# A decayed linear attention with an MLP behind it: batch 0's diagonal sums as products on TensorE, its decay tables by doubling, a tiled U^T x, and a planner that starts each engine at its own time

## The chip, the cores and the metric

The kernel runs on one core of a Trainium2 chip. The metric is the device time of one execution in microseconds (us); the median of three runs of the kernel before is 419.65 us (419.59 to 420.86). One execution was also taken by the hardware profiler, and all rows of the profile come from that one.

TensorE is called PE below, VectorE DVE, ScalarE ACT, GpSimd POOL and SyncE SP, as in the profile. SP and ACT issue the DMAs.

## The reference

Two stages follow each other. The first is a linear attention with a decaying state, for 4 batches, 8 heads, 768 time steps and a head size of 48:

```python
for t in range(S):
    kt, vt, rt = (k[:, :, t], v[:, :, t], r[:, :, t])
    cur = np.einsum('bhd,bhe->bhde', u[None] * kt, vt)
    y[:, :, t] = np.einsum('bhd,bhde->bhe', rt, state + cur)
    state = w[None, :, :, None] * state + np.einsum('bhd,bhe->bhde', kt, vt)
```

The term with `u` is the diagonal: the row t of y gets v_t times the number sum_d r_t[d] u[d] k_t[d], one such number for each head and step.

The second stage takes x, the attention's result with the heads side by side (768 rows of 384 per batch), adds a mixing over time of rank 32, and an MLP of width 1536:

```python
xt = x.transpose(0, 2, 1)
h = xt @ U @ V
u = x + h.transpose(0, 2, 1)
ch = np.maximum(u @ w_ch1, 0.0) @ w_ch2
return (u + ch).astype(np.float32)
```

All arithmetic is float32. The four arrays of the second stage arrive as 64-bit floats, seen by the kernel as pairs of 32-bit words.

## The kernel before, in words

**Attention.** The 768 steps of a batch are cut in 6 chunks of 128 rows, a chunk in two halves of 64. Heads go in pairs: a pair's 2 x 48 channels lie on partitions 0 to 47 and 64 to 111 (PD = 112 rows). For a chunk n, r and k are loaded row by row (`a_load`), turned by PE (`a_tr`, 128x128 transposes into a PSUM bank, tiles `ptr` and `ptk`) and scaled by tables of powers of w as they are copied out (rT on DVE, kT on DVE or ACT). `ks` is k times another table, `tab` (`a_ks`). A chunk is computed in two parts (`a_part`): each has 64x64-tiled matmuls of the chunk n itself (`pav`: masked scores `am` times v, and rT times the state S) interleaved with those of the chunk n + 1 (`pab`: scores, and the state's increment). Part 1 may start when ACT or DVE has read one element of part 0's bank (`seen`). Between parts DVE masks the scores (`am`, L967), adds the increments into the state (`S`, L995), and somebody multiplies the state by the decay (`SW`, L1004 or L1008). So chunk n + 1 cannot start its part 0 before part 1 of chunk n, its `am` and its `S`, and before rT and kT of chunk n + 2 are there. The very first matmuls (`a_first`) are the scores and increments of chunk 0 alone.

The diagonal is computed beside it: r times k, times `ub` (u on all partitions), each a 128x384 product (`a_dv`, L713 and L715, on POOL for batch 0), a sum over the 48 channels on DVE (`a_dg`, L721), and v times that sum with 8 small ACT instructions a chunk (L725). `a_x` (L974) adds it to the bank of `pav` and gives x.

**Tables.** w is loaded transposed, 4 bytes at a time (`load_w`, L415 and L417), clipped, and powers of it and of its reciprocal are built on DVE (`tables`, L437 to L460). One of them, `tw`, is turned by PE (L465) and becomes `tab` (L467).

**From x to the MLP.** For batch 0, `c_gx` adds each chunk's U^T x to columns 128 to 511 of the PSUM bank `wake`, with three full 128x128 matmuls a chunk that use three copies of U side by side; `c_g0` splits the sum into high and low parts (`Gs`). For the other batches `c_g` does the whole sum in one go, with 24 matmuls on four 32-column tiles (`pG`, L1040; a float32 product leaves two rows in the trace, so 48), and gathers the four blocks by four small copies first. `c_x` turns x into the banks `pu`, `c_xu` adds V^T Gs there, and ACT and DVE split the result into `uTh` and `uTl`.

**MLP.** For a block of 384 rows and a slice f of 128 hidden channels, `m_1` has 9 matmuls of 384 columns (three split products by three 128-row pieces), ACT takes relu into `hh` (L1162), DVE the rest into `hl` (L1163), and `m_2` has 9 more. Batch 0's slices go in the order t0 f0-3, t1 f0-7, t0 f4-11, t1 f8-11, since the weights come in meanwhile. Each weight slice, 64-bit, has to be converted: 8 bits of exponent by DVE (L540) or ACT (L544), the rest scaled by ACT (L566), sign and join on DVE (L547, L550), a high part by ACT (L584), a low part by DVE or POOL (L585). The last stores of `out` are issued by `m_2` (L1207).

**The order of the work.** Nothing is left to a compiler: each step is an `op` with an engine (or several to choose from, `one_of` and `on_either`), a cost in ns, what it reads and writes, and a key. The key is a due time in us that the code at the end of `rwkv_moe` gives (`T0` and `PER` for the MLP, `FRONT` and `EACH` for batch 0's chunks). `Plan.schedule` simulates the engines with these costs, picks among what is ready the smallest key, and so fixes the order of every engine's queue; at run time each engine works through its queue in order and waits on semaphores. Where PE would be idle, the plan fills in matmuls of an identity (`wake`), so that PE's clock stays up; they sit in the queue too, ahead of what follows.

While batch b is in its MLP, the attention of batch b + 1 is woven between its matmuls. Only batch 0's attention has nothing to be woven into.

Of the kernel before, what the change touches and what calls it, by code (L numbers as in the profile page):

```python
# [20 lines left out]
W_LO = 0.7  # L21
# [26 lines left out]
class Plan:  # L48
# [7 lines left out]
    LANDS = 1650  # L56

    CROWD, CROWDED = 1.29, 32000
# [20 lines left out]
    def op(self, eng, ns, fn, w=(), r=(), alt=(), lock=False, dma=0.0, rows=0, late=0.0, tiled=False, dk=0.0):  # L79
# [11 lines left out]
        for acc, write in [(a, False) for a in r] + [(a, True) for a in w]:  # L91
            b, sub = acc if isinstance(acc, tuple) else (acc, None)
            if not b.uses and b.tag:
                o.allocs.append(b)
                ring = self.rings.setdefault(b.tag, {"order": [], "next": 0, "free": [(0.0, "")] * b.bufs, "last": None})
# [53 lines left out]
    def schedule(self):  # L149
        free = dict.fromkeys(self.AFTER, 0.0)  # L150
# [49 lines left out]
        while left:  # L200
            best = None
            for e, cs in cands.items():
# [9 lines left out]
                for t, o, i in sorted((a for a in at if a[0] <= now + 1), key=lambda a: a[1].key):  # L212
# [13 lines left out]
            if e == "PE":  # L226
                for begin, end, filler in self.wakes:
# [4 lines left out]
                    while self.pe_end(x, begin.ways[0][1], 0, False) < t - 150:  # L232
# [46 lines left out]
def dve(n):  # L279
    return 130 + 1.09 * n  # L280
# [11 lines left out]
def rwkv_moe(ctx: ExitStack, tc: tile.TileContext, r, k, v, w, u, U, V, w1, w2, out):  # L292
# [20 lines left out]
    NR = 2  # L313
    NK = 2
# [75 lines left out]
    wT = cbuf([PD, NP, 1], F32, "wT")  # L390
# [3 lines left out]
    tabT = cbuf([PD, 2, NP, C2 + 2], F32, "tabT")  # L394
    wi = cbuf([PD, NP, 1], F32, "wi")
    wm = cbuf([PD, NP, 1], F32, "wm")
    tab = cbuf([128, DM], F32, "tab")

    Uf = cbuf([128, NCH, 3, R], F32, "Uf")
# [14 lines left out]
    def load_w():  # L414
        dma(lambda q: q.dma_start(wT.t[:HP, :, 0], bass.AP(tensor=w.tensor, offset=w.offset, ap=[[1, HP], [2 * D, NP]])),  # L415
            [(wT, 0)], [], HP * NP, 4, ns=730)
        dma(lambda q: q.dma_start(wT.t[HP:, :, 0], bass.AP(tensor=w.tensor, offset=w.offset + D, ap=[[1, D], [2 * D, NP]])),  # L417
            [(wT, 1)], [], D * NP, 4, ns=580)
# [4 lines left out]
    def table(i):  # L423

        return tabT.t[:, i, :, i:i + C2].unsqueeze(2).broadcast_to([PD, NP, 2, C2])
# [4 lines left out]
    def tables():  # L430

        HC = C2 // 2
        NS = HC.bit_length()
        sq = cbuf([PD, 2, NP, NS], F32, "sq")
        tt = tabT.t
        pw = tt[:, :, :, HC:C2]
        on_dve(4, lambda e: e.tensor_scalar(wT.t, wT.t, W_LO, W_HI, ALU.max, ALU.min), [wT], [])  # L437
        op("POOL", 500, lambda: nc.gpsimd.memset(pw[:, :, :, 0:1], 1.0), [tabT], [])
        on_dve(4, lambda e: e.tensor_copy(sq.t[:, 0, :, 0:1], wT.t), [sq], [wT])
        for i in range(1, NS):  # L440
# [1010 lines left out]
```

## Time and profile before

| | us |
|---|---|
| median of three runs | 419.65 |
| the profiled execution's own time | 420.94 |
| span of its trace, first to last instruction | 419.1 |
| first matmul of attention (`a_first`) | 12.07 |
| part 0 of the last chunk of batch 0 | 42.78 |
| first matmul of the MLP | 52.39 |
| last matmul of the MLP ends about | 413.2 |
| PE busy, of the span | 408.1 (97%) |
| DVE busy | 263.9 (63%) |
| ACT busy | 134.8 (32%) |
| POOL busy | 74.6 (18%) |

How to read it: the two times of the second and third row are of one execution, and 1.84 us lie around the span. Busy time of PE counts the `wake` matmuls, which compute nothing. The time marks in the middle are starts of instructions in the chain of work that ended last. A row of the view by windows gives a stretch, its length, then the busy time and the number of instructions of PE, PE's weight loads, DVE, ACT and POOL, the granted clock of PE (1.00 is full), a share of DMA time, and GB/s. A row of a timeline or of the chain gives start, length, engine, line and tile.

### The profile page before, as it was taken

To read this page: it belongs to the slowest core of one execution; us is meant where nothing else is said; L and a number is where in the kernel's file an instruction comes from. 1 tells how busy PE (TensorE), PEld (TensorE's weight loads), DVE (VectorE), ACT (ScalarE), POOL (GpSimd) and SP (SyncE) were. 2 spreads that over 40 slices of the span, in tenths; PEclk is the share of its full clock that TensorE was granted. 3 is DMA by queue.
4 is the path that set the end of the run, shared out by engine and by line. 5 is a ranking of instruction groups with operands and counts; after the bars stand their busy time and mean duration, and the time that the engine had idled before them with its cause. 6 is when DMAs were issued, how large, how long until landed. Compare 5 with 4: busy or idle time off the path is not lost.

```text
span 419.1 us, 12257 instructions
## 1 busy us (share of the span) xinstructions
PE 408.1 (97%) x5164; PEld 393.3 (94%) x5164; DVE 263.9 (63%) x594; ACT 134.8 (32%) x358; POOL 74.6 (18%) x114
## 2 busy tenths in 40 slices
PE   8998999999999999999999999999999999999994
PEld 8887999999999898999999999999999999999993
DVE  6878998889898559877784358866523361122122
ACT  2467967547641415212113130112113121111110
POOL 2642150145621103321000003321000000000000
PEclk9999999999999999999999999999999999999998
DMA  9978969899557677755677814520100510001001
GB/s 145 149 160 256 201 163 242 125 224 234 94 85 154 142 144 132 149 103 87 137 140 107 152 68 64 101 39 2 59 2 0 114 57 2 0 2 58 2 0 61
DMA packets 181951, 43.53 MB, mean 104 GB/s; under 512 B 168961, under 2 KB 180354, under 8 KB 181890
## 3 DMA queue, kind: packets, MB, share of 16 engines
q1 hardware_dynamic: 176706, 41.21, 49.1%
q10 hardware_dynamic: 5184, 1.48, 2.0%
q8 instruction: 42, 0.69, 0.7%
q14 instruction: 19, 0.16, 0.1%
HBM read 36.18 MB, written 6.49 MB: 102 GB/s over the span
## 4 chain that ended last, share of the span: by engine, by line
PE 91%; DVE 4%; ACT 2%; issue 1%; POOL 0%; DVEq 0%; ACTq 0%; POOLq 0%
PE p L347 72%; PE wake L347 3%; PE pav L836 3%; PE pav L842 3%; PE pab L795 3%; PE pab L810 2%; PE pu L347 2%; PE ptk L756 1%; PE pG L1040 1%; PE pav L821 1%; DVE am L967 1%; PE ptr L756 1%; ACT dv L725 1%; DVE SW L1004 1%; DVE ut L1136 1%
## 5 line engine op out<-in xcount | busy, mean ns | idle before, releaser
L347 PE MATMUL p<-uTh,w1s 128*128 128x384 f32 x576 | 147.5, 336 | 0.0
L1163 DVE SCALAR_TENSOR_TENSOR hl<-p,hh 128x384 fp32r<-128x384 f32 x96 | 53.2, 555 | 114.9 <-ACT hh L1162 114.5
L347 PE MATMUL p<-w2s,hh 128*128 128x384 f32 x576 | 119.9, 340 | 0.5 <-ACT hh L1162 0.4
L1162 ACT ACTIVATE hh<-p 128x384 fp32r<-128x384 f32 x96 | 47.2, 491 | 222.8 <-PE p L347 220.2
L347 PEld LDWEIGHTS p<-uTh,w1s 128*128 128x128 f32 x576 | 103.2, 188 | 0.5
L347 PEld LDWEIGHTS p<-w2s,hh 128*128 128x128 f32 x576 | 100.0, 188 | 2.4 <-ACT hh L1162 1.1
L347 PE MATMUL p<-uTl,w1s 128*128 128x384 f32 x288 | 96.5, 335 | 0.0
L347 PE MATMUL p<-w2s,hl 128*128 128x384 f32 x288 | 66.1, 335 | 0.0
L347 PEld LDWEIGHTS p<-uTl,w1s 128*128 128x128 f32 x288 | 54.0, 188 | 0.3 <-DVE uTl L1095 0.3
L347 PEld LDWEIGHTS p<-w2s,hl 128*128 128x128 f32 x288 | 51.4, 188 | 0.1
L795 PE MATMUL pab<-rT,kT 48*64 48x64 f32 x768 | 30.6, 223 | 1.8 <-issue 1.0
L836 PE MATMUL pav<-vsw,am 64*64 64x48 f32 x384 | 30.4, 222 | 0.1
L842 PE MATMUL pav<-S,rT 48*64 48x48 f32 x704 | 29.5, 218 | 0.0
L836 PEld LDWEIGHTS pav<-vsw,am 64*64 64x64 f32 x384 | 25.2, 134 | 1.9 <-issue 1.0
L795 PEld LDWEIGHTS pab<-rT,kT 48*64 48x64 f32 x768 | 24.9, 134 | 2.1 <-ACT dv L725 0.8
L842 PEld LDWEIGHTS pav<-S,rT 48*64 48x64 f32 x704 | 25.8, 135 | 0.0
L836 PE MATMUL pav<-ldv,am 64*64 64x48 f32 x320 | 24.2, 221 | 0.0
L705 POOL MEMSET ks<- 128x128 f32 x24 | 4.9, 204 | 101.9 <-PE pav L842 57.0
L967 DVE TENSOR_TENSOR am<-pab,mask 128x256 f32<-128x256 f32 x48 | 19.4, 417 | 5.4 <-PE pab L810 3.9
L836 PEld LDWEIGHTS pav<-ldv,am 64*64 64x64 f32 x320 | 20.2, 134 | 2.5 <-issue 2.1
L810 PE MATMUL pab<-ldv,ks 64*48 64x48 f32 (+1 forms) x576 | 21.1, 212 | 0.0
L995 DVE TENSOR_TENSOR S<-pab,SW 112x192 f32<-112x192 f32 x40 | 14.0, 351 | 8.2 <-PE pab L810 5.5
(136 smaller groups left out, 520.2 us busy)
## 6 DMA issues: line engine op xcount, KB each, us to landing
raw_w<-in_moe_w_ch_dram SPq DMA_DIRECT2D x24, 384.0 KB, 4.7
out_dram<-x SPq DMA_DIRECT2D x21, 192.0 KB, 2.4
ldr<-in_r_dram SPq DMA_DIRECT2D x20, 192.0 KB, 3.1
ldk<-in_k_dram SPq DMA_DIRECT2D x20, 192.0 KB, 3.5
ldv<-in_v_dram SPq DMA_DIRECT2D x20, 192.0 KB, 3.9
bl<-in_r_dram SPq DMA_DIRECT2D x79, 48.0 KB, 2.6
bl<-in_k_dram SPq DMA_DIRECT2D x79, 48.0 KB, 2.4
vsw<-in_v_dram SPq DMA_DIRECT2D x42, 48.0 KB, 2.7
```

Of the source, the lines that this page charges most:

```text
L347: return nc.tensor.matmul(*args, **kw)
L705: op("POOL", 250, lambda: nc.gpsimd.memset(ks.t[:, :, D:], 0.0), [(ks, "pad")], [])
L725: nc.scalar.activation(dv.t[:, h], vt()[:, h], AF.Copy, scale=dg.t[:, h:h + 1])
L756: nc.tensor.transpose(pt.t[:, q * C:(q + 1) * C], src().rearrange("p h d -> p (h d)")[:, q * PE_:(q + 1) * PE_], ident_)
L795: return [lambda q=q, i=i: nc.tensor.matmul(pt.t[(i ^ j) * C2:(i ^ j) * C2 + C2, q * C2:(q + 1) * C2], lhsT=kT.t[rows, q, i * C2:(i + 1) * ...
L810: return nc.tensor.matmul(pt.t[j * HP:j * HP + m, SU + q * D:SU + (q + 1) * D], lhsT=ks.t[half, 2 * q + j, :m], rhs=vt()[half, 2 * q + j, ...
L836: return nc.tensor.matmul(to(q, j, i), lhsT=am[j].t[half, q, :], rhs=vsw[n].t[half, q, :] if j else vt()[half, 2 * q, :], start=((i == 1 i ...
L842: return nc.tensor.matmul(to(q, row, i), lhsT=rT.t[rows, q, i * C2:(i + 1) * C2], rhs=St[n, i].t[rows, q, :], start=False, stop=((alone or ...
L967: on_dve(256, lambda e: e.tensor_tensor(am.t, abs_[n][j].t[:, :SU].rearrange("p (h t) -> p h t", h=NP), mask_.unsqueeze(1).broadcast_to([1 ...
L995: on_dve(192, lambda e, new=new, ptv=ptv, dec=decayed[n, j]: e.tensor_tensor(new.t, ptv(), dec.t, ALU.add), [new], [pt, decayed[n, j]])
L1162: on_act(384, lambda: nc.scalar.activation(hh.t, pt.t[:, :TB], AF.Relu), [hh], [pt])
L1163: on_dve(384, lambda e: e.scalar_tensor_tensor(hl.t, pt.t[:, :TB], 0.0, f32(hh.t), ALU.max, ALU.subtract), [hl], [pt, hh])
```

## The change

1. **Diagonal sums (batch 0).** `a_rk` multiplies rT by kT (both already turned and scaled, so that the scales cancel up to one power of w) on DVE, and four PE matmuls with 2 columns each sum it over the channels against `u2`, which holds u times w. The sums land in free columns of the `wake` bank. `a_diag` copies them out and scales v by them, on ACT or on DVE. r times k, times ub, and DVE's sum fall away for batch 0; `ub` is loaded later.
2. **Tables.** w and u come in as four rows each and are turned by PE. The powers 1 to 64 are built by doubling in six products; `tw` is read from the same powers backwards. kT of chunk 0 now comes from `ks`, like that of the others.
3. **Engines.** `ks` of chunks 2 to 5 goes to POOL, that of chunks 0 and 1 stays on DVE. The decay `SW` of batch 0 may go to POOL or ACT, no longer to DVE.
4. **U^T x.** Batch 0's is done like the others', on four 32-column tiles: chunks 0 to 3 at once, then 4 and 5; `c_g0` is gone. U is kept once, not three times.
5. **Plan.** Each engine begins at a time of its own; a held instruction may be preferred to a later one if the engine would wait little; there are somewhat fewer `wake` matmuls; the costs of DVE, of transposes in `c_turn` and of a last part are others; PER is 1.85 for 1.95; batch 0's preparation is due 3 us earlier; U and V are converted at 32 and 38 instead of both at 32; a weight's conversion is due 2 us ahead of its use instead of 6; k is loaded ahead of r and v; the flag's load waits for the last weight.
6. **End.** The middle one of the three last stores is issued by SP instead of ACT.

The diff, cut to its core:

```diff
+    BEGINS = {"DVE": 900, "ACT": 800, "PE": 1650, "POOL": 1000, "SP": 800}
+    SPARE = 0.15
-    CROWD, CROWDED = 1.29, 32000
+    CROWD, CROWDED = 1.2, 32000
+    HOLD, HELD = 3, 50000
...
-        free = dict.fromkeys(self.AFTER, 0.0)
+        free = dict(self.BEGINS)
...
+                    while e != "SP" and t < self.HELD:
+                        held = [(u, p, k) for u, p, k in at if p.key[0] < o.key[0] - self.HOLD and len(p.ways) == 1 and u > t + 1
+                                and 2 * (u - t) < o.ways[i][1] - self.OVERLAP[e] - 60]
+                        if not held:
+                            break
+                        t, o, i = min(held, key=lambda a: a[0])
...
-                    while self.pe_end(x, begin.ways[0][1], 0, False) < t - 150:
+                    until = t - 150 - (min(self.SPARE * (t - x), 600) if self.clock(x) == 1 else 0)
+                    while self.pe_end(x, begin.ways[0][1], 0, False) < until:
...
 def dve(n):
-    return 130 + 1.09 * n
+    return 163 + 1.02 * n
...
+    def load_pairs(a, t):
+        for i, (c0, c1) in enumerate(((0, HP), (HP, PD))):
+            dma(lambda q, i=i, c0=c0, c1=c1: q.dma_start(t.t[:, c0:c1], bass.AP(tensor=a.tensor, offset=a.offset + i * D,
+                                                                              ap=[[2 * D, NP], [1, c1 - c0]])),
+                [(t, i)], [], NP, 256, ns=500)
...
+        while m < C2:
+            on_dve(4 * m, lambda e, m=m: e.tensor_mul(p[:, :, m + 1:2 * m + 1], p[:, :, 1:m + 1],
+                                                      p[:, :, m:m + 1].broadcast_to([PD, NP, m])), [(pw, 1)], [])
+            m *= 2
...
-                  only="DVE" if front(n) else None)
+                  only="DVE" if n < KS else "POOL" if front(n) else None)
+
+    def a_rk(n):
+
+        rT, kT = trs[n]
+        rk = xbuf([PD, NP, C], F32, "hh", NH, f"rk_{n}")
+        on_either(512, lambda e: e.tensor_mul(rk.t, rT.t[:PD], kT.t[:PD]), [rk], [rT, kT], only="DVE" if n < RK else "POOL")
+        at_ = RKCOL + 2 * NP * n
+
+        def sums():
+            for q in range(NP):
+                whole(wk.t[:, at_ + 2 * q:at_ + 2 * q + 2], lhsT=rk.t[:, q, :], rhs=u2.t[:, q, :], start=False, stop=True,
+                      skip_group_check=True)
+        pe(480, sums, [(wk, f"d{n}")], [rk, u2])
+
+    RKCOL, RK, DIAG = 256, 6, 6
+
+    def a_diag(n):
+        vt, vb = vs[n]
+        dv = dvs[n] = xbuf([128, H, D], F32, "hh", NH, f"dv_{n}")
...
+        if n < DIAG:
+            one_of([("ACT", 1900, small, False),
+                    ("DVE", dve(384), lambda: nc.vector.tensor_mul(dv.t, vt(), dg.t.unsqueeze(2).broadcast_to([128, H, D])), True)],
+                   [dv], vb + [dg])
+            return
...
-               alt=[("DVE", dve(192), lambda one=one: one(nc.vector), True), ("ACT", NP * (act(D) - 94) + 94, four, False)])
+               alt=([] if front(n) else [("DVE", dve(192), lambda one=one: one(nc.vector), True)]) +
+               [("ACT", NP * (act(D) - 94) + 94, four, False)])
...
+    def g_sum(pt, c0, ns):
+
+        w4 = DM // 4
+        for n in ns:
+            for g in range(4):
+                nc.tensor.matmul(pt.t[g * R:(g + 1) * R, c0:c0 + w4], lhsT=Uf.t[:, n % NCH, 0],
+                                 rhs=xs[n].t[:, g * w4:(g + 1) * w4],
+                                 start=(c0 == 0 and n % NCH == 0), stop=(n % NCH == NCH - 1), skip_group_check=True)
+
+    def c_gx(*ns):
+
+        return pe(170 * len(ns), lambda: g_sum(wk, 128, ns), [(wk, "g")], [Uf] + [xs[n] for n in ns], tiled=True)
...
-                        128, 1536, ns=375, eng="ACT" if b == B - 1 and t == NTB - 1 else "SP")
+                        128, 1536, ns=375, eng="ACT" if b == B - 1 and t == NTB - 1 and i != 1 else "SP")
...
-    T0, PER = 46.0, 1.95
+    T0, PER = 46.0, 1.85
+    UV, GX, UVC = -84.9, (3, 38.6), (32.0, 38.0)
...
-        at((T0 + use[i] * PER - 6 if i > 1 else -14 + T0) + 0.01 * i, convert)
+        at((T0 + use[i] * PER - 2 if i > 1 else UVC[i]) + 0.01 * i, convert)
...
-    end = attention(0, FRONT, EACH, 1.0, 0)
+    end = attention(0, FRONT, EACH, 4.0, 0)
```

More of the change, by code (lines that the diff above doesn't have):

```diff
@@ L423, in table @@
     def table(i):
-        return tabT.t[:, i, :, i:i + C2].unsqueeze(2).broadcast_to([PD, NP, 2, C2])
+        return (tabT.t[:, :, ::-1] if i else tabT.t).unsqueeze(2).broadcast_to([PD, NP, 2, C2])
     def subs(ap):
@@ L432, in tables @@
         HC = C2 // 2
[L433 to L440, printed above, removed]
-            on_dve(4, lambda e, i=i: e.tensor_mul(sq.t[:, 0, :, i:i + 1], sq.t[:, 0, :, i - 1:i], sq.t[:, 0, :, i - 1:i]),
-                   [sq], [])
@@ new lines, in rwkv_moe, with small @@
+    RKCOL, RK, DIAG = 256, 6, 6
+    def a_diag(n):
+        vt, vb = vs[n]
+        dv = dvs[n] = xbuf([128, H, D], F32, "hh", NH, f"dv_{n}")
+        at_ = RKCOL + 2 * NP * n
+        dg = dgs[n] = wbuf([128, H], F32, "dg", 2, f"dg_{n}")
+        one_of([("ACT", 160, lambda: nc.scalar.copy(dg.t, wk.t[:, at_:at_ + H]), False),
+                ("DVE", 167, lambda: nc.vector.tensor_copy(dg.t, wk.t[:, at_:at_ + H]), False)], [dg], [(wk, f"d{n}")])
+        def small(h0=0, h1=H):
+            for h in range(h0, h1):
+                nc.scalar.activation(dv.t[:, h], vt()[:, h], AF.Copy, scale=dg.t[:, h:h + 1])
+        if n < DIAG:
[3 more added lines that the diff above has]
+            return
+        for h in range(0, H, 2):
+            op("ACT", 560, lambda h=h: small(h, h + 2), [(dv, h)], vb + [dg])
@@ L709, in a_dv @@
     def a_dv(n):
+        if front(n):
+            a_rk(n)
+            return
         (rt, rb), (kt, kb) = rs[n], ks_[n]
-        dv = dvs[n] = (xbuf([128, H, D], F32, "hh", NH, f"dv_{n}") if front(n) else
-                       wbuf([128, H, D], F32, "dv", 2, f"dv_{n}"))
-        on_either(384, lambda e: e.tensor_mul(dv.t, rt()[:, :, :D], kt()[:, :, :D]), [dv], rb + kb,
-                  only="POOL" if front(n) and n else None)
-        on_either(384, lambda e: e.tensor_mul(dv.t, dv.t, ub.t), [dv], [ub], only="POOL" if front(n) and n else None)
+        dv = dvs[n] = wbuf([128, H, D], F32, "dv", 2, f"dv_{n}")
@@ L725, in small @@
                 nc.scalar.activation(dv.t[:, h], vt()[:, h], AF.Copy, scale=dg.t[:, h:h + 1])
-        if front(n):
-            for h in range(0, H, 2):
-                op("ACT", 560, lambda h=h: small(h, h + 2), [(dv, h)], vb + [dg])
-            return
         one_of([("ACT", 1900, small, False),
@@ L747, in a_tr @@
         src, sb = (ks_ if i else rs)[n]
-        if i and n:
+        if i:
             ks = kss[n]
@@ L910, in a_part @@
         if part == 0:
-            pe(600 if last else 1000, first, wr, rd, tiled=True)
+            pe(950 if last else 1000, first, wr, rd, tiled=True)
             t = wbuf([128, 1], F32, "seen", 2, f"seen_{n}")
@@ L921, in a_part @@
         else:
-            pe(600 if last else 1000, second, wr, rd + [seens[n]], tiled=True)
+            pe(950 if last else 1000, second, wr, rd + [seens[n]], tiled=True)
         if nxt:
@@ L1389, in rwkv_moe @@
             end = attention(b, t0, per, 5.0, 0)
-        at(end, lambda b=b: c_g(b) if b else c_g0())
+        at(end, lambda b=b: c_g(b))
         if b == 0:
```

132 lines of the change are left out of this document (68 added, 64 removed).

## The prediction

> **What bounds the kernel now.** I began with the page (PE busy 97%, DVE 63%), which says little, since part of PE's work in the front is `wake`, which computes nothing. So I cut the span at the marks that the chain of waits gives, and asked the view by windows (columns: stretch, its length, then busy time and count of PE, PE's weight loads, DVE, ACT, POOL; granted clock; a DMA share; GB/s).
>
> ```profile
> 12.07:42.78 30.71, 27.97 (x779) 24.81 (x779) 24.12 (x59) 21.60 (x83) 14.10 (x24) 1.00 0.88 192
> 42.78:52.39 9.61, 9.61 (x121) 9.02 (x122) 9.00 (x19) 8.86 (x22) 1.77 (x2) 1.00 0.91 193
> 52.39:80.00 27.61, 27.61 (x163) 27.17 (x163) 26.36 (x55) 18.76 (x46) 8.17 (x10) 1.00 0.89 183
> 52.39:413.30 360.91, 360.12 (x4192) 349.21 (x4191) 221.70 (x482) 101.96 (x253) 56.17 (x76) 1.00 0.46 92
> 413.30:419.10 5.80, 0.00 (x0) 0.00 (x0) 0.43 (x1) 0.00 (x0) 0.00 (x0) 0.68 0.31 107
> ```
>
> From 52.39 on PE is idle for 0.8 us in 361, and the change takes no matmul out of that stretch. It can only be moved as a whole. So the question is how much earlier the MLP's first matmul starts, plus what the last 5.8 us give. The 52.39 us ahead of it are batch 0's attention. The chain of waits shows its last part, and PE's timeline where the chunks' parts begin:
>
> ```profile
> 12.07 0.62 PE pab L795 x32
> ...
> 41.71 0.36 DVE V L605
> ...
> 42.30 0.44 DVE am L967
> ...
> 42.78 0.67 PE pav L836 x16
> ...
> 43.91 1.92 PE wake L347 x16
> 45.83 0.60 PE pav L836 x16
> ...
> 48.70 0.90 PE wake L347 x7
> ...
> 50.82 1.10 PE pu L347 x6
> ...
> 52.39 7.77 PE p L347 x43
> ```
>
> ```profile
> 15.22 0.31 PE L836 MATMUL pav<-vsw,am 64*64 64x48 f32 x2
> ...
> 31.39 0.31 PE L836 MATMUL pav<-vsw,am 64*64 64x48 f32 x2
> ...
> 33.25 0.25 PE L836 MATMUL pav<-ld,am 64*64 64x48 f32 x1
> ...
> 36.03 0.31 PE L836 MATMUL pav<-vsw,am 64*64 64x48 f32 x2
> ...
> 39.02 1.51 PE L347 MATMUL pv<-raw_v,sel 128*96 128x192 f32 x8
> ```
>
> Part 0 of the first chunk starts at 15.22 and that of the sixth at 42.78: 27.56 us for five chunks, 5.5 each; from the fourth (31.39) to the fifth (36.03) it is 4.64, from there to the sixth 6.75. In that last one PE spreads V for 1.51 us ahead of a part, and `am` comes at 42.30 behind V's split on DVE. In the front no engine is full: DVE 79% and ACT 70% of 30.71. From 42.78 to 52.39 both are (94% and 92%), with the conversion of the weights.
>
> **The change, part by part.** *The start.* DVE's, ACT's and POOL's timelines (POOL's row is for the rule below):
>
> ```profile
> 4.57 0.17 DVE L437 TENSOR_SCALAR wT<-wT 112x4 f32<-112x4 f32 x1 [1.95 <-DMA wT<-in_w_dram]
> ...
> 4.98 0.97 DVE L441 TENSOR_TENSOR sq<-sq 112x4 f32<-112x4 f32 x5
> ...
> 8.06 0.69 DVE L457 TENSOR_TENSOR tw<-tabT,wm 112x512 f32<-112x512 f32 x1
> ...
> 15.72 1.32 DVE L1004 TENSOR_TENSOR SW<-S,wm 112x192 f32<-112x192 f32 x1
> ...
> 23.91 0.35 DVE L1004 TENSOR_TENSOR SW<-S,wm 112x192 f32<-112x192 f32 x1
> ...
> 30.83 0.69 DVE L765 TENSOR_TENSOR rT<-ptr,tabT 112x512 f32<-112x512 f32 x1 [0.30 <-PE ptr L756]
> ...
> 34.81 0.35 DVE L995 TENSOR_TENSOR S<-pab,SW 112x192 f32<-112x192 f32 x1
> ...
> 46.94 0.56 DVE L974 TENSOR_TENSOR x<-pav,dv 128x384 f32<-128x384 f32 x1 [0.47 <-PE pav L842]
> ```
>
> ```profile
> 10.08 0.48 ACT L467 COPY tab<-pt_tab 128x384 f32<-128x384 f32 x1 [6.15 <-PE pt_tab L465]
> ```
>
> ```profile
> 15.81 1.00 POOL L713 TENSOR_TENSOR dv<-ld 128x384 f32<-128x384 f32 x1
> ```
>
> w lands for DVE at 4.57 and `tw` is done at 8.75: 4.2 us. After: a clip and six products, five like the 0.194 us ones of L441 and two of up to 128 elements (0.3), then `tw` at 0.69: about 2.25 us, so 1.9 less. The load of w has 16 short rows (8 of w, 8 of u) for 448 pieces of 4 bytes, and DVE waited 1.95 us for it; but the loaded rows now go through PE first, and the one such step in these rows, from `tw` (8.75) to `tab` (10.08), took 1.33. I set the two as equal. From `tab` (10.56) to `a_first` (12.07) is 1.5 us now; kT of chunk 0 is now behind `ks` (0.55), four transposes (0.6) and a copy (0.68 on DVE): 2.0 with the hops, 0.3 to 0.5 more. Sum: **-1.5 us**; bounds +0.5 (nothing gained up to `tab`, and the longer way behind it) and -2.5 (the load gains 1). From there to the first part 0 (15.22) I leave the 3.15 us as they are.
>
> *Chunk to chunk.* What a chunk cannot go below is in the rows: part 0 to part 1 is 1.86 (31.39 to 33.25), part 1 to its last `S` another 1.9 (33.25 to 35.16), so 3.8. What it takes above that, 0.9 to 1.7, is mostly rT: at 30.83 it starts only behind its transposes, which PE did after the part; due 3 us earlier, they can go between the parts. The groups of the stretch 12.07 to 52.39 tell what each engine has to carry (busy, mean ns of one):
>
> ```profile
> L765 DVE TENSOR_TENSOR rT<-ptr,tabT 112x512 f32<-112x512 f32 x5 | 3.4, 682 | 0.3 <-PE ptr L756 0.3
> L721 DVE TENSOR_REDUCE dg<-dv 128x8 f32<-128x384 f32 x6 | 3.2, 541 | 0.0
> L1004 DVE TENSOR_TENSOR SW<-S,wm 112x192 f32<-112x192 f32 x5 | 3.5, 704 | 0.0
> L725 ACT ACTIVATE dv<-ld,dg 128x48 f32<-128x48 f32 x32 | 8.1, 326 | 3.6 <-DVE dg L721 3.5
> L715 POOL TENSOR_TENSOR dv<-dv,ub 128x384 f32<-128x384 f32 x5 | 5.5, 1094 | 0.2
> L706 DVE TENSOR_TENSOR ks<-ldk,tab 128x384 f32<-128x384 f32 x2 | 1.3, 645 | 0.0
> L771 ACT ACTIVATE kT<-ptk,wi 112x128 f32<-112x128 f32 x16 | 4.6, 367 | 1.5 <-PE ptk L756 1.5
> ```
>
> DVE loses six sums (3.2), four `ks` (4 x 0.6 = 2.4) and five `SW` (3.5), and gains six `rk` of rT's size (6 x 0.68 = 4.1): -5.0 us. ACT gains six copies of the sums (at most 0.33 each, like its other small ones) and perhaps two of the `SW` (four such each): +2 to +5. POOL loses ten products of 1.0 to 1.1 and gains four `ks` and `SW`: it is not the bound. So the diagonal is no longer work for POOL, and its sum no longer DVE's; the saving on DVE and ACT together is only 0 to 3 us, of which I take 2. The larger effect is that `seen` and rT wait less, and that V's spread (1.51) and split no longer lie ahead of parts. `rk`'s sums are 8 more rows on PE a chunk; between the tiled rows of `pG` (0.024 each, below) and the `wake` rows (0.12) that is 0.2 to 1.0 us, where PE runs `wake` matmuls now. If that cover is gone it costs up to 6 us, and it stands in the range.
>
> I take 4.8 us a chunk, nearest to the 4.64 of the undisturbed fourth, because ACT (dv 2.0, kT 1.1, `seen`, copies, `SW`) gets near 4.4. 5 x 4.8 = 24.0 for 27.56: **-3.6 us**; bounds -6.5 (4.2 a chunk) and +1 (5.7).
>
> A rule to weigh: at 15.72 one `SW` on DVE took 1.32 us while POOL ran a product (15.81), at 23.91 the same took 0.35, where POOL's timeline has no row. `rk` is a product of two SBUF tiles too, and POOL's `ks` runs beside it. If one in two collides at the 0.97 us seen here, that is 3 x 0.97 = 2.9 us on DVE, against 1.75 us of collisions that go with the `SW` (3.5 less five of 0.35); the 1.2 between them is inside what I leave open on DVE, and half a term of the range. The Trainium skill, "GPSIMD Engine Reference", section "8. Key points", says that GpSimd shares its SBUF interfaces with VectorE and contends with DVE instructions that have two SBUF inputs; the trace agrees with these two rows.
>
> *Last chunk to the MLP.* Between part 0 (42.78) and part 1 (45.83) of the last chunk are 3.05 us, of which 1.92 are U^T x; undisturbed it was 1.86. **-1.2.** At the end, Gs:
>
> ```profile
> 142.17 1.17 PE pG L1040 x48
> ...
> 145.68 0.76 PE pu L347 x3
> ```
>
> In batch 1 the tiled sum of six chunks takes 1.17 us, and from its end (143.34) to the next step (145.68) go 2.34 with the four copies. For chunk 5 alone: 0.2 + 2.34 = 2.5. Now the same is 0.90 of PE from 48.70 and 1.22 to 50.82, 2.1, but that started 1.2 after x was ready (DVE's x ends about 47.5). 50.82 - 47.5 = 3.3 against 2.5 and a hop: **-0.4**, with -1.0 and +0.5 as bounds.
>
> *The weights.* They are what comes late next. DVE and ACT carried 33.1 + 30.5 = 63.6 us in the 40.3 us from 12.07 to 52.39 (79%); with 2 less it is 61.6. With the three terms above the MLP would start at 45.7, from a start at 10.6: 35.1 us, 88%. That is tighter, but the stretch 42.78 to 52.39 ran at 93%, and a part of the conversion can go into 52.39 to 80.00, where ACT has 8.9 us and POOL 19 us idle though DVE has 1.3. I charge **+1.2**, bounds 0 and +4.
>
> *The tail.*
>
> ```profile
> L1207 ACTq DMA_DIRECT2D out_dram<-x x3: 372/389/1210, 412.7 to 414.5; - x3
> ...
> 412.13 1.60 DVE L1202 TENSOR_TENSOR x<-p,x 128x384 f32<-128x384 f32 x3 [1.00 <-PE p L347]
> ```
>
> The last store is issued at 414.5, though its x is done at 413.73, behind the second's issue of 1.21. On another queue it can go at once: 0.8 less, but the second itself then ends near 414.4 as before: **-0.6**, bounds 0 and -0.8.
>
> Sum: -1.5 - 3.6 - 1.2 - 0.4 + 1.2 - 0.6 = -6.1 us. The profiled execution took 420.94 (span 419.1 and 1.84 around it), so 414.8 for it; it lies 1.3 above the median of the runs, and on the median 419.65 the sum gives 413.5. What a measurement of this kernel can tell from no change is about 0.3%, 1.3 us.
>
> **The rivals.** *The conversion holds it.* DVE and ACT may be no better packed than now. 61.6 us at 79% of two engines are 39.0 us; from 10.6 the MLP starts at 49.6, 2.8 earlier; with the tail 3.4 gained: 416.2. For it: 94% and 92% ahead of 52.39, and conversions due 4 us later than before. Against it: the first stretch is not full, and its gaps are waits that the change addresses. Chance 0.22.
>
> *The chunks run at their floor.* 4.0 a chunk (-7.6) and no charge for weights: -11.3, 408.4. For it: the fillers and rT that go away; against: ACT near 4.4 a chunk. Chance 0.08.
>
> *PE's clock falls (slower).* The change thins the `wake` matmuls and replaces 36 full-array U^T x rows of 0.12 by short ones. The last row of the windows shows the granted clock at 0.68 once PE stands idle; everywhere else it is 1.00, as PE is kept busy. At half clock the two parts of a chunk (1.1 to 1.4 each by the rows at 31.39 and 33.25) take 2.5 us longer; from the third cold chunk on that eats the 6.1 us, and with four it is +3.9: 423.6. For it: less filling; against: the plan's own model counts PE's work per stretch, and thins only where the clock is up. Chance 0.05. The Trainium skill, "TensorE: Matmul & The Clock Gate", section "What's actually happening", states the rule that speaks against thinning: half rate is the default state, restored after an idle window of about 3.4 us. By that rule only idle stretches of that length would do it, and PE's whole idle time in the second row of the windows, 2.74 us, is below it.
>
> *It gives back what it gains (no change).* `rk` and its sums lie ahead of parts on DVE and PE, and the MLP waits for the weights by as much as it starts earlier: 0.5 to 1 us gained at the tail alone, 419. Chance 0.05.
>
> **How the numbers follow.** Forecast 0.60, the rivals 0.22, 0.08, 0.05 and 0.05. The forecast's own range, by its terms' bounds without all of them at once, is 410 to 416.5. To hold 8 in 10 it takes in the held conversion and reaches to 417.5; below, 409.5. Faster by over 1.3 us: 0.60 + 0.22 + 0.08 = 0.90. Within: 0.04 of the case that gives back; its other 0.01, and the clock's 0.05, are slower, 0.06.
>
> **What would show it.** Right: `tw` done near 6.5, the first `pab` near 10.6, sixth part 0 near 37, the first MLP matmul near 46, PE idle below 2 us behind it, last store issued before 414 less the shift. Wrong: parts 5.5 us apart still, with `rk` or ACT's dv ahead of `seen`; PE idle in the MLP's first 25 us waiting for `w1s` or `w2s`; a granted clock below 1.00 before the end; a stretch behind the MLP's start other than 361 us.

## The result and the profile after

The kernel after took 425.83 us (median of four runs, 425.02 to 431.32), the kernel before 420.25 beside it (419.59 to 422.28): 1.6% slower, ratio 1.0158 (95% interval 1.0122 to 1.0195). The profiled execution took 425.93, its span is 424.2, for 420.94 and 419.1 before. Ratios are formed without runs that lie over 1.5% above the fastest of their kernel; as the kernels with the change scatter by more than that through PE's clock, medians of all runs are compared below.

The view by windows of the kernel after, cut at the first `pab`, part 0 of the last chunk, the MLP's first matmul and its last one:

```profile
11.35:44.53 33.18, 30.74 (x797) 27.82 (x799) 21.97 (x56) 17.30 (x68) 11.17 (x24) 0.80 0.81 195
44.53:58.45 13.92, 13.22 (x116) 10.81 (x116) 7.76 (x16) 7.18 (x18) 6.32 (x6) 0.61 0.56 103
58.45:418.50 360.05, 359.79 (x4192) 348.90 (x4191) 224.97 (x487) 103.14 (x259) 52.77 (x72) 1.00 0.46 91
418.50:424.20 5.70, 0.10 (x1) 0.00 (x0) 0.69 (x2) 0.00 (x0) 0.00 (x0) 0.69 0.31 111
```

The stretch behind the MLP's start is as long as before (360). The loss is all in front of it: the MLP starts at 58.45 and not at 52.39. And no engine beside PE is full there: from 44.53 to 58.45 DVE is busy for 7.76 us of 13.92 (94% in the same stage before). The odd column is the last but two: a granted clock of 0.80 and 0.61 where the kernel before had 1.00. A finer cut shows where it falls:

```profile
25.00:29.00 4.00, 4.00 (x128) 3.57 (x129) 2.68 (x7) 2.77 (x13) 2.36 (x7) 1.00 0.70 151
29.00:30.00 1.00, 0.47 (x34) 0.53 (x25) 1.00 (x3) 0.93 (x5) 1.00 (x2) 1.00 1.01 365
30.00:32.00 2.00, 0.10 (x2) 0.10 (x1) 0.96 (x4) 0.08 (x1) 0.84 (x3) 0.88 0.74 258
32.00:40.00 8.00, 8.00 (x147) 7.26 (x147) 3.02 (x9) 4.08 (x16) 0.92 (x3) 0.50 0.84 262
40.00:50.00 10.00, 10.00 (x141) 8.28 (x141) 5.60 (x13) 5.04 (x13) 0.00 (x0) 0.50 0.69 129
50.00:55.00 5.00, 5.00 (x51) 4.12 (x50) 2.05 (x6) 1.90 (x6) 4.70 (x6) 0.50 0.10 19
55.00:58.45 3.45, 2.75 (x16) 2.34 (x16) 3.34 (x6) 2.91 (x8) 1.61 (x1) 0.94 0.90 158
```

PE stops between 29.5 and 31.9, and from 32 to 55 it runs at half clock, though it is shown busy all the time. The stop, in the timeline of PE's weight loads (in brackets the idle time ahead of a row and what ended it):

```profile
29.39 0.19 PEld L359 LDWEIGHTS wake<-u,rk 112*128 112x128 f32 x1
31.90 1.57 PEld L359 LDWEIGHTS wake<-u,rk 112*128 112x128 f32 x7 [2.32 <-issue]
```

"issue" means that PE waited for nothing that the profile shows. At that time the MLP's weights are loading (DMA at 365 GB/s in 29 to 30). Until then the front was faster, as the starts of part 0 of the first and fourth chunk show (15.22 and 31.39 before):

```profile
15.40 0.31 PE L889 MATMUL pav<-vsw,am 64*64 64x48 f32 x2
...
28.32 0.25 PE L889 MATMUL pav<-vsw,am 64*64 64x48 f32 x1
```

These are 4.31 us a chunk and a lead of 3.1 us. The chain of waits then shows how it is lost:

```profile
11.35 0.69 PE pab L848 x32
...
44.53 1.02 PE pav L889 x16
46.41 2.80 PE pv L359 x8
49.69 1.02 PE pav L889 x16
...
57.17 1.28 PE pu L359 x6
58.45 7.03 PE p L359 x39
```

The spread of V, eight rows `pv`, took 1.51 us before and takes 2.80 at half clock; the first 16 `pav` rows of a part 1.02 for 0.60 to 0.67.

### The profile page after: what moved, and what is told of

It reads as the page before. It is cut to its first block, busy times and chain, and to the rows that moved or that the text cites. A ratio compares the mean times of both kernels' runs of the same rounds, so it can differ in the third digit from the quotient of the medians.

```text
span 424.2 us, 12169 instructions
## 1 busy us (share of the span) xinstructions
PE 412.5 (97%) x5137; PEld 395.0 (93%) x5137; DVE 261.6 (62%) x583; ACT 130.1 (31%) x347; POOL 71.9 (17%) x115
## 4 chain that ended last, share of the span: by engine, by line
PE 95%; DVE 2%; ACT 1%; issue 1%; POOL 0%; DVEq 0%; POOLq 0%
PE p L359 73%; PE pav L889 4%; PE pav L895 4%; PE pab L848 3%; PE wake L359 3%; PE pu L359 2%; PE pab L863 2%; PE ptk L809 1%; PE ptr L809 1%; PE pG L1076 1%; PE pav L874 1%; PE pv L359 1%; PE wake L1076 1%; PE ph L359 0%; DVE pw L467 0%
## 5 line engine op out<-in xcount | busy, mean ns | idle before, releaser
L359 PE MATMUL p<-w2s,hh 128*128 128x384 f32 x576 | 117.6, 337 | 0.0
L848 PE MATMUL pab<-rT,kT 48*64 48x64 f32 x768 | 32.1, 229 | 0.4 <-DVE kT L830 0.4
L889 PE MATMUL pav<-vsw,am 64*64 64x48 f32 x384 | 32.0, 230 | 0.0
L895 PE MATMUL pav<-S,rT 48*64 48x48 f32 x704 | 31.4, 228 | 0.0
L889 PEld LDWEIGHTS pav<-vsw,am 64*64 64x64 f32 x384 | 26.9, 143 | 2.1 <-issue 1.2
L895 PEld LDWEIGHTS pav<-S,rT 48*64 48x64 f32 x704 | 27.7, 145 | 0.0
L848 PEld LDWEIGHTS pab<-rT,kT 48*64 48x64 f32 x768 | 26.1, 139 | 1.5 <-DVE kT L830 0.7
L889 PE MATMUL pav<-ldv,am 64*64 64x48 f32 x320 | 25.9, 229 | 0.0
L889 PEld LDWEIGHTS pav<-ldv,am 64*64 64x64 f32 x320 | 21.8, 142 | 1.3 <-issue 1.3
```

The source lines that it names most:

```text
L359: return nc.tensor.matmul(*args, **kw)
L848: return [lambda q=q, i=i: nc.tensor.matmul(pt.t[(i ^ j) * C2:(i ^ j) * C2 + C2, q * C2:(q + 1) * C2], lhsT=kT.t[rows, q, i * C2:(i + 1) * ...
L889: return nc.tensor.matmul(to(q, j, i), lhsT=am[j].t[half, q, :], rhs=vsw[n].t[half, q, :] if j else vt()[half, 2 * q, :], start=((i == 1 i ...
L895: return nc.tensor.matmul(to(q, row, i), lhsT=rT.t[rows, q, i * C2:(i + 1) * C2], rhs=St[n, i].t[rows, q, :], start=False, stop=((alone or ...
```

## The experiments

The questions were, in this order: is the slower time a matter of single runs; which part of the change takes the clock away; what holds it; and where the rest of the forecast gain is, once it is held. The before time beside each run was 420.08 to 420.13.

**again.** The kernel after, unchanged.

> The changed kernel once more, for another trace of it. In the first trace PE stood still from 29.4 to 31.9 us while the weights were being loaded, then its granted clock was 0.50 from 32 to 55 us. Theory A (PE waits for its own instructions, whose fetch lies behind the weights' loads; the clock falls for that idle): the stall comes again while raw_w lands, 1 to 3 us long; the clock falls only in those runs where the stall is long enough, so that the mean clock and the span vary from run to run (0.968 to 0.996 so far), median near 425.8. Theory B (the thinned wake matmuls let the clock fall): the clock falls in every run at the same place, with or without a stall ahead of it.

Measured: 428.94 (417.13 to 430.25, four runs). Its view by windows:

```profile
10.00:18.00 8.00, 7.44 (x105) 6.83 (x107) 5.66 (x16) 0.37 (x2) 2.18 (x4) 0.62 0.95 187
...
30.00:35.00 5.00, 1.80 (x71) 1.66 (x71) 3.08 (x8) 2.30 (x10) 2.61 (x6) 1.00 0.90 294
35.00:58.00 23.00, 23.00 (x335) 19.66 (x335) 11.64 (x28) 11.95 (x36) 6.62 (x9) 0.52 0.59 124
```

The same program: the clock now falls twice, also at 12 to 18 us, and the stop is 3.1 us of "issue". One run of four, with a mean clock of 0.994, took 417.13. So the time of this kernel is a matter of when PE's clock falls, and all eight runs of it (417.13 to 431.32) have a median of 427.1. Neither theory holds as it stands: the stop came again, as A says, but the first of the two falls, near 12, lies 20 us ahead of it; and the falls do not come at one place in every run, as B would have it.

**full_fill.** This takes back the thinning of `wake` that the diff names:

```diff
-    SPARE = 0.15
+    SPARE = 0.0
```

> The changed kernel with SPARE at 0, so that the plan fills PE's gaps with wake matmuls as it did before the change. Theory B: the clock stays at 1.00, the MLP starts near 46 us, 413 to 416 us. Theory A: the stall while raw_w lands is still there and nothing fills it, since PE has no instructions to run; the result stays within 2 us of the changed kernel, 424 to 428.

Measured: 425.86 (421.45 to 431.43, ten runs), trace at clock 0.50 from 35 to 55. This is A's time and not B's 413 to 416, but the run did not put the filling back: its trace has 26 `wake` rows (two a matmul), against 24 in the kernel after. So it says that the thinning rule is not what took the `wake` away, and nothing yet on what the loss of `wake` does. Nor does it bear out A's long stop: "issue" in front of PE lasts 0.9 us here and ends at 30.24, PE is busy again from there on, and the clock still falls to 0.50 at about 31.5. The count itself was the discovery. The view of the tile `wake`, identity rows up to 46 us, before and after:

```profile
L347 PE MATMUL wake<-ident x112: 274/275/582, 1.7 to 38.9; 128*128 128x128 f32 x112
```

```profile
L359 PE MATMUL wake<-ident x24: 421/421/582, 1.6 to 36.7; 128*128 128x128 f32 x24
```

56 matmuls of the identity before, 12 after (a float32 product leaves two rows). The plan fills idle time that it foresees on PE, and in the new front it foresees hardly any; which of the plan's changes does that was not tried one by one. Also, a median row takes 421 ns for 275. At 36.7, where the clock column says 0.50, a row takes these 421 ns too, so this is half clock, and it is there already in the first microseconds, where the column still says 1.00.

**one_ahead.** One weight load in flight instead of three:

```diff
-    AHEAD = 3
+    AHEAD = 1
```

> The changed kernel with AHEAD at 1: a weight's load is issued only when the one before it has landed, so that one is in flight and not three. Theory A: PE's stall between 27 and 34 us shrinks below 1 us and the clock stays at 1.00, or falls in fewer runs; the MLP starts near 47 to 50 us, if anything held by the weights, which now come every 3 to 4 us; 415 to 421. Theory B: the clock falls as before, 424 or more.

Measured: 433.37 (428.57 to 440.05). PE does not stop near 30, and the clock is 1.00 from 25 to 50; but it is 0.50 at 10 to 20, and from 50 to 62 PE waits for the weights (6.78 us busy of 12) and it falls again (0.57). With fewer loads in flight the stop near 30 is gone; the stop is not the only thing that lowers the clock.

**old_diag.** The diagonal as before, all else as after: no two-column rows of rk on PE, r times k and times ub on POOL again, sums, `ks` and some `SW` on DVE:

```diff
-        if front(n):
-            a_rk(n)
-            return
...
-        if front(n):
-            a_diag(n)
-            return
```

> The changed kernel with the diagonal sums of batch 0 computed the old way (r times k times ub on POOL, the sum on DVE, v times it on ACT by pairs of heads, ks on DVE, the decay allowed on DVE again); tables, tiled U^T x, the plan's new rules and the last store stay as changed. 11 wake matmuls. Theory C: the wake matmuls are as few, so the clock falls here too and the runs spread, median 422 to 430. Theory D (the 48 two-column rows of rk's sums are what lets the clock fall): the clock stays at 1.00, 414 to 419.

Measured: 431.46 (430.78 to 432.18). The windows:

```profile
10.00:20.00 10.00, 7.44 (x132) 6.33 (x135) 7.70 (x18) 4.27 (x17) 3.66 (x6) 0.56 1.45 169
...
30.00:40.00 10.00, 8.52 (x243) 7.07 (x244) 9.23 (x25) 8.02 (x27) 5.15 (x10) 0.70 0.91 277
```

The rows of rk are not needed for the fall: without them, and with 11 `wake` matmuls, the clock falls too, and the kernel is 4 to 6 us slower still.

**before_thin.** The kernel before, its filling loop thinned from 56 `wake` matmuls to 8, nothing of the change:

```diff
-                    while self.pe_end(x, begin.ways[0][1], 0, False) < t - 150:
+                    while self.pe_end(x, begin.ways[0][1], 0, False) < t - 980:
```

> The kernel before with 8 wake matmuls in its front instead of 56, nothing else of the change. Theory C: its clock falls too, at 10 to 20 us or behind 30 us, the mean clock goes from 0.997 to 0.96 to 0.98, the times spread as those of the changed kernel do (over 5 us between runs), 423 to 432. Theory A: as the weights' loads lie where they lay, the clock stays and the time with it, 418 to 421.

Measured: 430.81 (429.84 to 431.67), ratio 1.0245 (1.0213 to 1.0277), first MLP matmul at 61.39.

```profile
L347 PE MATMUL wake<-ident x16: 421/421/582, 1.7 to 29.9; 128*128 128x128 f32 x16
...
L347 PE MATMUL wake<-x,Uf x4: 417/417/417, 38.6 to 39.2; 128*96 128x128 f32 x4
```

Taking `wake` out of the kernel before costs 10.7 us, with rows at half rate: the rows of U^T x above take 417 ns, in the kernel before 273 (median). So the loss of `wake` alone is enough to make a kernel slower by more than the change did. The clock column does not show it: it says 1.00 up to 60 us, and the mean clock of this execution, 431.67 us, is 0.993; in two others of the four runs it is 0.964. A mean near 1 is thus no proof that PE ran at full rate.

**fill_more.** The reverse, on the kernel after:

```diff
-                    until = t - 150 - (min(self.SPARE * (t - x), 600) if self.clock(x) == 1 else 0)
+                    until = t + 200 if t > x + 80 else x
```

> The changed kernel with 39 wake matmuls in the front instead of 12 (the kernel before has 56): one is put into every gap of over 80 ns that the plan sees, even if it holds the next step up by 200 ns. Theory C (the clock falls because the plan's shorter front leaves almost no wake matmuls, and tiled and two-column matmuls do not count as enough work for the clock): the clock is 1.00 far more of the time, mean above 0.985 in most runs, the MLP starts near 46 to 48 us, 414 to 418. Theory A (the wait for instructions alone makes it fall): wake matmuls are instructions too, and more of them make the fetch worse; 424 or more.

Measured: 421.58 (419.9 to 427.35, ten runs), with 39 `wake` matmuls and a mean clock of 0.981 to 0.996. It gains 4 to 5.5 us, though C's 414 to 418 is missed. PE still stops, for 1.4 us up to 32.05, now without the clock falling there; it falls to 0.83 in 50 to 60, behind waits ahead of `pu`, the longest 2.0 us, which the view puts down to ACT's conversion of a weight.

**fill_early.** The rule of fill_more only where the plan's time is below 15 us:

```diff
+                    if x < 15000:
+                        until = t + 200 if t > x + 80 else x
```

> The kernel after, with the fuller rule of wake matmuls (up to the next matmul plus 0.2 us, for every planned gap of over 0.08 us) only where the plan's time is below 15 us; later gaps keep the rule of the kernel after, and the weights load as there. Theory 'early gaps': the run's time is decided by the thin filling ahead of 15 us; then this kernel comes within 1.5 us of fill_more (421.6), with a clock of 0.99 or more. Theory 'stall': the clock goes up early but is lost at PE's stop near 29 to 32 us, and the later wake matmuls are what fill_more gained by; then 424 to 427 with a granted clock of 0.5 from about 32 to 55 us in the trace.

Measured: 425.9 (419.71 to 429.51, six runs), 32 `wake` matmuls for the 39 of fill_more; the profiled execution is the fastest of the six, and even there the clock is 0.83 from 30 to 40. "Early gaps" fell: most of what fill_more gained hangs on a few matmuls behind 15 us. The time is the one that "stall" gives; its sign, 0.5 from 32 to 55, does not stand in this one trace.

**late_weights.** The kernel after; the first three weight loads wait for the masked scores of chunk 5 (an added dependency on its `am`):

```diff
+    GO = (5, 0)
...
-                    if before:
-                        tc.add_manual_dep(mine[0].ins, before[0][0].ins.name,
+                    if before or big_one:
+                        tc.add_manual_dep(mine[0].ins, (before[0][0] if before else masked[GO]).ins.name,
...
-        at(UV + 0.01 * i if i < 2 else -50 + 0.1 * i if i < 2 + EARLY else T0 + use[i] * PER - 6 - LEAD, load)
+        at(UV + 0.01 * i if i < 2 else 34.0 + 0.1 * i if i < 2 + EARLY else T0 + use[i] * PER - 6 - LEAD, load)
```

> The changed kernel with the first three weight loads waiting for the mask of the scores of chunk 5 (am), so that no weight is loaded while batch 0's chunks run. Theory A: no stall over 0.5 us of PE ahead of that point, the clock 1.00 all through, part 0 of the sixth chunk near 37 us; then the MLP waits for the weights and starts at 47 to 51 us: 416 to 420. Theory B: the clock falls near 31 us as in the changed kernel, the sixth part 0 comes after 42 us, and the total is 428 or more since the weights come later as well.

Measured: 423.54 (417.92 to 427.57, ten runs). No stop in 30 to 40 and clock 1.00 from 40 on in the trace, but 0.50 at 10 to 20. The time lies between those of the two theories.

**fill_late.** The edits of fill_more and late_weights together.

> The changed kernel with 39 wake matmuls, and with the first weight loads waiting for the mask of chunk 5's scores, so that neither of the two supposed causes is left. Theory C with A as the trigger near 30 us: clock 1.00 from 10 us on in nearly all runs, spread below 3 us; the MLP is held by the weights as in late_weights and starts near 49 us: 417 to 420. If the clock still falls in half of the runs, neither is the cause.

Measured: 419.55 (418.91 to 421.5, ten runs), ratio 0.9988 (0.9969 to 1.0006), a clock of 0.994 or more in every run, and the scatter is gone. So the two make a square of medians: with thin filling 427.1 (loads early) and 423.54 (late), with full filling 421.58 and 419.55. Filling is worth 4 to 5.5 us, the later loads 2 to 3.5.

**before_late.** The kernel before with the edit of late_weights on its loads, `GO = (4, 0)`, due at 31.

> The kernel before with the same edit on the loads: the first three weight loads wait for the masked scores of chunk 4, all else unchanged. It tells whether the later loads would help the kernel before as well, so that fill_late's time says nothing for the change. Theory 'the loads alone': PE's stop of 1.1 us in 36 to 38 us goes and the MLP does not wait for weights: 418.5 to 419. Theory 'no gain without the change': the stop moves with the loads or the weights come late for the MLP, which starts at 52.4 as before: 419.7 to 421.

Measured: 419.98 (419.53 to 421.71), ratio 1.0007 (0.9991 to 1.0022). PE's stop in 36 to 38 goes (4.97 us busy of 35 to 40, for 3.94), but the time does not move. What fill_late gains over the kernel after is not a gain that the kernel before could have too.

**fill_go4, fill_go3.** fill_late with the weights one and two chunks earlier, `GO = (4, 0)` due at 28.5 and `GO = (3, 0)` due at 23.

> fill_late, but the first three weight loads wait for the masked scores of chunk 4 instead of chunk 5, one chunk (about 4.3 us) earlier. Theory 'the clock is all that was lost': PE no longer waits for weights behind 50 us (0.9 us in 55 to 60 in fill_late), the MLP starts near 49, the clock stays at 0.99 or more: 417.5 to 418.5, 0.4 to 0.6% below the kernel before. Rival 'loads under the chunks stop PE': a stop of 1 us or more of PE with 'issue' in front of it comes back while the loads overlap the chunks, part of the runs have a lower clock: 421 to 423.

> fill_late with the first three weight loads behind the masked scores of chunk 3, two chunks (about 8.6 us) earlier than in fill_late and near where the kernel after issues them. Theory 'the clock is all that was lost': the weights are early enough for the MLP and the rest as in fill_go4: 417 to 418.5. Rival 'loads under the chunks stop PE': the stop of PE is back as in fill_more (1.4 us near 32 us), the clock falls in part of the runs: 420.5 to 423, as fill_more (421.6).

Measured: 421.1 (419.04 to 424.29) and 422.21 (420.71 to 423.15). The rival is right on the time: the versions with earlier weights are slower, not faster, stops of 1.0 to 1.1 us with "issue" are back, and in fill_go3 the clock is 0.84 in 30 to 40. But in fill_go3 the stop ends at 27.2, ahead of the weights' issue at 28.3, so there it is not the weights that are in flight. In fill_go4 the two largest waits of PE's weight loads from 35 to 60 are (total, times, longest):

```profile
PEld p L359 <- DVE uTl L1148: 2.2, 1, 2.2
PEld wake L1079 <- issue: 1.3, 2, 1.1
```

The first line is new: DVE, busy with conversion, is late with the MLP's own input. Earlier weights do not make an earlier MLP.

**Where the gain is when the clock is held.** In fill_late, the chain of waits:

```profile
39.65 0.60 PE pav L892 x16
...
40.71 1.52 PE pv L359 x8
...
42.54 0.60 PE pav L892 x16
...
49.78 1.20 PE p L359 x7
50.98 2.66 DMA ldr<-in_r_dram
53.66 2.23 DVE raw_w L568 x2
55.89 1.29 DVE raw_w L571
```

and its windows:

```profile
15.48:39.58 24.10, 24.02 (x737) 21.99 (x736) 17.57 (x47) 15.08 (x64) 9.46 (x20) 1.00 0.47 107
...
49.62:411.70 362.08, 360.58 (x4193) 349.12 (x4191) 229.27 (x491) 106.74 (x271) 54.12 (x74) 1.00 0.47 96
```

Five chunks take 24.1 us, but the span is only 1.3 us shorter than before. V's spread lies between the last two parts, and seven matmuls into the MLP the chain leaves PE: a load's landing, then DVE's conversion of the next weights. Two places in PE's queue looked as if they cost time. In the kernel after the sums of rk stand ahead of the next chunk's transposes:

```profile
12.43 1.05 PE L359 MATMUL wake<-u,rk 112*128 112x2 f32 x8
13.34 0.63 PE L809 MATMUL ptr<-ident,ld 128*128 128x128 f32 x4
13.81 0.60 PE L809 MATMUL ptk<-ident,ks 128*128 128x128 f32 x4
```

On fill_late, **rk_late** makes rk due later, **v_late** V's conversion, **both_late** has both, and **both_go** also lets the loads go behind the second half of chunk 4's scores:

```diff
-            at(t + 0.2 * i, f)
+            at(FRONT + EACH * n - 1.0 if f is fs[3] and front(n) else t + 0.2 * i, f)
...
-    UV, GX, UVC = -84.9, (3, 38.6), (32.0, 38.0)
+    UV, GX, UVC = -84.9, (3, 38.6), (32.0, 40.0)
...
-    GO = (5, 0)
+    GO = (4, 1)
```

> fill_late with rk and its sums due 1 us ahead of the chunk's part 0 instead of right behind its transposes: on PE the sums of chunk 0 stand behind the transposes of chunk 1, not ahead. Theory 'the place in the queue': the first part 0 starts at 14.5 to 14.8 instead of 15.48, the marks behind it shift by the same, 418.6 to 419.0. Rival 'the weights hold the end': the part starts shift but PE waits for weights behind 50 us by as much more: 419.5, as fill_late.

> fill_late with V's conversion due at 40 instead of 38, so that its spread on PE (1.52 us between the two parts of the last chunk) stands half between and half behind them. Theory 'the place in the queue': part 1 of the last chunk starts about 0.75 us earlier (2.1 behind part 0 instead of 2.9) and the MLP starts 0.5 earlier: 419.0. Rival 'the weights hold the end': no change in the time, 419.5.

> The edits of rk_late and v_late together, on fill_late. Theory 'the place in the queue': the gains add, 418.0 to 418.5, an MLP start near 48.4. Rival 'the weights hold the end': MLP start earlier, PE's waits for weights in 50 to 60 above 2 us, 419.5.

> both_late, and the first weights wait for the second half of the masked scores of chunk 4 instead of the first half of those of chunk 5, about 2 us earlier. Theory 'the place in the queue': the weights are no longer late, 417.0 to 418.0. Rival 'loads under the chunks stop PE': a stop of about 1 us with 'issue' ahead of it as in fill_go4, 420 to 421.

Measured: 419.95 (419.44 to 420.4), 420.35 (419.57 to 421.36), 420.34 (419.63 to 422.71) and 419.33 (419.0 to 419.86). "The place in the queue" fell. In rk_late the sums do stand behind the transposes, yet part 0 starts at 15.83, later than 15.48. DVE now stands waiting for the sums, and six `wake` rows wait for DVE's copy out of the bank `wake`:

```profile
14.74 0.17 DVE L752 COPY dg<-wake 128x8 f32<-128x8 f32 x1 [0.66 <-PE wake L359]
```

```profile
14.97 0.94 PE L359 MATMUL wake<-ident 128*128 128x128 f32 x6 [0.26 <-DVE dg L752]
15.83 0.25 PE L892 MATMUL pav<-vsw,am 64*64 64x48 f32 x1
```

The wait went from PE to DVE, and the filling came on top: in the chain part 0 follows these six rows, though `am`, rT and kT were done by 14.6. In v_late part 1 follows part 0 after 2.2 us for 2.9 and the MLP starts 0.4 earlier, but PE then waits 3.3 us from 48 on for `w1s`, `w2s` and x on DVE. "The weights hold the end" gave the time of all three within 0.9 us. both_go met neither number (417 to 418, or 420 to 421), but its mechanism is the first: PE is busy for 9.95 us of 50 to 60, 8.75 in fill_late. It is the one version whose interval lies below the kernel before: ratio 0.9976 (0.9962 to 0.9991), 0.2%.

## Why the prediction was wrong

Forecast were 413.5 us in 409.5 to 417.5; measured 425.83. By the marks of the chain, in us against the kernel before (fill_late is the change with the clock held):

| step | forecast | after | fill_late |
|---|---|---|---|
| to the first part 0 | -1.5 | +0.2 | +0.3 |
| five chunks, part 0 to part 0 | -3.6 | +1.6 | -3.4 |
| last chunk, part 0 to part 1 | -1.2 | +2.1 | -0.2 |
| from there to the MLP | +0.8 | +2.2 | +0.7 |
| MLP to its last matmul | 0 | -0.6 | +1.2 |
| behind it | -0.6 | -0.4 | +0.1 |
| span | -6.1 | +5.1 | -1.3 |

**The clock, the step that failed.** The prediction named this rival with its mechanism and a price of 423.6 "with four cold chunks", and gave it 0.05. Against it stood that "the plan's own model counts PE's work per stretch, and thins only where the clock is up". The runs show that this reasoning looked at the wrong line of the diff: the thinning rule changes next to nothing (full_fill), while the plan's filling went from 56 matmuls to 12 with the new front. That the loss of fillers alone leaves PE at half rate is shown by the rows of before_thin, and that restoring most of them raises the clock by fill_more. What was missing was a count: the fillers per stretch in the trace, and what in the new order would take their place. The prediction counted the `wake` rows as cover that the sums of rk could use up for nothing; in the kernel before they were what kept the clock.

The second argument was the size of idle stretches: PE's idle time of 2.74 us in a window of the kernel before (it is the first row's, 30.71 less 27.97; the second row, which the prediction names, has none). The Trainium skill, "TensorE: Matmul & The Clock Gate", section "What's actually happening", gives an idle window of about 3.4 us for the fall and as much sustained work for the return. The trace does not agree with either: the clock fell behind a stop of 2.3 us, and it stayed at 0.50 for 23 us in which PE is shown busy without a gap. The length of the stop does not decide either: behind 0.9 us in full_fill the clock fell, behind 1.4 us in fill_more it did not. Neither a sum of idle time nor its longest piece is a measure here.

**The first part 0.** The tables came as forecast: the clip, the six products and `tw` on DVE, then `tab` on ACT (8.26 for 10.08):

```profile
4.70 0.17 DVE L463 TENSOR_SCALAR pw<-pt_w 112x4 f32<-112x4 f32 x1 [2.93 <-PE pt_w L462]
4.90 1.39 DVE L467 TENSOR_TENSOR pw<-pw 112x4 f32<-112x4 f32 x6
6.41 0.69 DVE L471 TENSOR_TENSOR tw<-pw 112x512 f32<-112x512 f32 x1
```

`tw` is done at 7.1 (forecast 6.5), the first `pab` starts at 11.35 (10.6), and the 3.15 us from there to part 0, which the prediction left as they are, became 4.05: the sums of rk take 1.05 us of PE there, the upper end of the 0.2 to 1.0 a chunk that the prediction gave, and rk_late shows that DVE waits for them if they come later. The mis-sized term is this one: the first diagonal is on the path, though no run shows an earlier part 0 without it. The clock has a part in the later `pab`: chunk 0's four transposes of k (`ptk`, at 9.48) take 1.09 us at half rate, 0.6 in the forecast. In fill_late they take 0.66, but there `pab` stands behind ten `wake` rows until 11.45.

**Chunk to chunk** was right where the clock was up: 4.31 us a chunk up to the stop, and 4.82 over all five in fill_late, for 4.8 forecast. But it was not ACT, at 4.4, that set it: in the kernel after PE is busy for all of 11.35 to 28.30, and in fill_late the chain from 15.5 to 39.7 is PE's alone. So the filling that holds the clock is now paid for on PE: the 22 identity rows of fill_late between the first part 0 and the last, at 0.11 us each (ten take 1.12 in the chain), are by estimate 2.5 us, about what its five chunks take above 5 x 4.31. The groups of the stretch 11.35 to 58.45 bear out the engines too:

```profile
L725 POOL TENSOR_TENSOR ks<-ldk,tab 128x384 f32<-128x384 f32 x4 | 5.4, 1343 | 0.0
L1057 POOL TENSOR_TENSOR SW<-S,wm 112x192 f32<-112x192 f32 x10 | 5.1, 507 | 6.5 <-DVE S L1048 6.5
L732 DVE TENSOR_TENSOR rk<-rT,kT 112x512 f32<-112x512 f32 x6 | 4.3, 721 | 0.1
```

rk on DVE averages 721 ns, 0.04 above the 0.68 assumed, so the collisions with POOL that the prediction weighed cost at most 0.2 us in six. All `SW` went to POOL here, none to ACT.

**Last chunk to the MLP.** U^T x did leave the place between the parts, and V's spread, which has a later due time, took it: 2.89 us for 3.05, not 1.86. The charge of 1.2 for the weights was right up to the MLP's start (+0.7 for +0.8), but another 1.2 came behind it, where PE waits for weights. So the rival "the conversion holds it", with its 416.2, is what remains when the clock is held, and it goes further than it did: fill_late measured 419.55, no gain that counts.

**The tail.** The last store is issued as soon as its x is done (419.2 in the kernel after, 412.3 in fill_late), as forecast. But from that issue to the end of the span go 5.0 and 5.5 us, for 4.6 before, so that of the 0.6 forecast 0.4 came in the kernel after and nothing in fill_late. Why was not looked into.

**What is not settled.** Why PE stops with "issue" was not tried by itself. Later or fewer weight loads take the stop near 30 away (late_weights, one_ahead), so they have a part in it, but fill_go3 has one ahead of them. The DMA's instruction queue q8 moves a packet of 16 KB (it moves 42 of them, 0.69 MB, in the whole span) in the microsecond ahead of the stop in the kernel after; that PE waits there for its own instructions is only a guess. Nor do the runs tell whether it is the small tiles or the two-column rows that leave the clock at half while PE is busy. One run of the kernel after, 425.02 at a mean clock of 0.996, looks out of place; it may have been at half rate where the column says 1.00, as before_thin was at 0.993, but no trace of that run shows it.

## What to carry to other kernels

Matmuls that compute nothing are work with a purpose: before an edit that shortens a stretch, count them by stretch in the trace and ask what keeps the clock up in the new order, as PE's busy share does not tell. If a kernel scatters by several per cent between runs and another does not, look at the granted clock of each run first, and at the duration of a row of known shape in its trace, as the clock column can miss a cold start. And a gain in front of a stage counts only up to what that stage waits for next: here it was the conversion of its weights, and in these runs the loads that feed it came with stops of PE when they were earlier.

## What the runs showed of the hardware

- PE's clock stayed at 0.50 from 32 to 55 us in the kernel after, while PE was shown busy for all of it with 64x64 tiles, two-column rows, 32-column tiles and transposes; in the kernel before it stayed at 1.00 with PE busy for 8.88 of 10 us (30 to 40).
- In these traces the clock column starts at 1.00, also where rows are at half rate. The rate of the first microseconds is read from a row of known shape: 421 ns for a 128x128 `wake` row at half clock, 275 at full. In before_thin the column says 1.00 up to 60 us while a row that takes 273 ns in the kernel before takes 417 at 39.2.
- With three loads of 384 KB in flight under the chunks, PE stopped for 0.9 us (full_fill), 1.1 (before), 1.4 (fill_more), 2.3 (after) and 3.1 (again) with no releaser shown; with the same loads 10 us later, in fill_late, no such stop is above 0.3. The clock fell behind the stops of 0.9, 2.3 and 3.1, and not behind those of 1.1 and 1.4.
- The same program took 417.1 to 431.3 us by where its clock fell.
